# First weights converted through PSUM, gated inputs and squared keys on ScalarE and GpSimd alone, attention output evicted by VectorE

## The chip, the cores and the metric

The kernel runs on one core of a Trainium2 chip. Its engines are TensorE (PE in the profile; PEld is its weight load), VectorE (DVE), ScalarE (ACT), GpSimd (POOL) and SyncE (SP), whose queue issues the DMAs. The metric is the device time of one execution in microseconds (us).

## The reference: what is computed

Three blocks follow each other, for batch 4, sequence 576 and model width 512.

- Attention with 8 heads of 64: rotary embedding of q and k, scores `q k^T / 8`, softmax, product with v.
- A gated feed-forward: with `x_prev` the input shifted by one position, `xk = mu_k*x + (1-mu_k)*x_prev` and `xr` alike with `mu_r`; `k = relu(xk @ w_k)`; `out = sigmoid(xr @ w_r) * ((k*k) @ w_v)`, with d_ff = 1024.
- A mixer: `u = x + (relu(x^T @ w_tok1) @ w_tok2)^T`, then `u + relu(u @ w_ch1) @ w_ch2`, with 256 token and 1536 channel features.

The weights w_k, w_v, w_r, w_tok and w_ch arrive as 64-bit floats; q, k, v and mu as 32-bit floats.

## The kernel before, in words

Every matrix product of 32-bit values is made of three matmuls: each operand is split into a high part in the matmul's own format and a low part, the rest, and high*high, high*low and low*high are summed (`mm3`, L527 to L532). So every operand needs one rounding copy and one subtraction. A 288-column half of the 576 positions is the moving operand in most products.

**Conversion of weights (`Conv`).** A weight is taken in chunks of 128 x 512 values, each two 32-bit words. Stage 0 loads the chunk by a DMA. Stage 1 has ScalarE write the absolute value of the high word into a work tile `cv` (L191). Stage 2 is four VectorE operations on it: clamp (L196), mask and shift (L198), sign and exponent bits out of the high word (L200), low bits out of the low word (L202). Stage 3 rounds on ScalarE (`parts`, L73) and subtracts (`parts`, L104) on the engine that `low` names. `conv0` does the 16 chunks of w_k and w_v beside the attention, `conv1` the 11 chunks of w_r and the token weights near the end of the attention, `conv2` the 24 chunks of the channel weights after it. One `step` issues stages for two chunks.

**Attention.** There are 16 groups (batch x pair of heads), each with 9 softmax tiles of 128 rows; tile j has the scores `S` (L362), the negated maximum `nm` (L368, DVE), the exp in place in PSUM (L375, ACT), the reciprocal of the sum (L382, L383, DVE), the probabilities as two 16-bit halves `p` (high on ACT, L75, low on DVE, L394), a DMA transpose (L411) and, for each of two units per group, the product with v (`pv`, L424). `out` (L433) evicts that product, scaled, from PSUM into `xT`. The rotary embedding of the next group's k (`rk`) and q (`rq`) is three elementwise steps each (`rope`), on DVE or POOL. `prep` issues it.

**Feed-forward (`kvr_gen`).** It starts once the first batch of attention is done and runs as a stream between the tiles of the later groups. A unit `K` is one batch and one half: `lerp_slice` makes the gated input in four slices (`a`, `f`, then `xs` high and low; the pools of `a` and `f` have one buffer each), eight products `kp` follow, each evicted with relu (`t`, L599), squared (`q`, L603), rounded (`k`, L80) and subtracted (`k`, L104), and then four products `vp` over all eight squared keys. A unit `R` does the gate for batch 0. `tok_gen` is the token mixing, `ch_gen` the channel mixing (`c1p`, `co`), `gate_gen` the gate of the later batches.

**Order.** The program is written as one stream; a scheduler with a timeline of its own and the priorities in `PRI` sets the order in which each engine's instructions stand. Each engine then runs its list strictly in that order. In POOL's list the 16 `words` memsets of `conv0` stand behind a rotary step and hold back the weight loads. The helper `copy` (L73 to L82) and `tt` (L104) record most elementwise work, so the profile tells such work apart by the names of the tiles and not by the line.

At two places the order of the change speaks for itself.

The first is VectorE's list in the second attention group, where `conv0` runs. `cv` and `cvp` are the work tiles of the conversion, `parts` the low half of a weight, `p16` the low half of the probabilities, `nm` the maximum. Before:

```order
L196 TENSOR_SCALAR cv_775<-cv_775 128x512
L202 SCALAR_TENSOR_TENSOR cv_683<-words_565,cv_683 128x512
L368 TENSOR_REDUCE nm_491<-S_478 128x1
L196 TENSOR_SCALAR cv_777<-cv_777 128x512
L308 TENSOR_REDUCE va_537<-vps_511 1x1
L104 TENSOR_TENSOR parts_889<-cv_681,parts_889 128x512
L198 TENSOR_SCALAR cv_775<-cv_775 128x512
L368 TENSOR_REDUCE nm_514<-S_501 128x1
L104 TENSOR_TENSOR parts_892<-cv_683,parts_892 128x512
```

With the change:

```order
L200 SCALAR_TENSOR_TENSOR cvp_578<-words_453,cvp_578 128x512
L402 SCALAR_TENSOR_TENSOR p16_622<-S_543,rc_618,p16_622 128x576
L376 TENSOR_REDUCE nm_616<-S_600 128x1
L335 COPY sc_609<-vps2_607 128x2
L203 SCALAR_TENSOR_TENSOR cv_583<-words_453,cvp_578 128x512
L376 TENSOR_REDUCE nm_637<-S_627 128x1
L390 TENSOR_SCALAR den_640<-S_600 128x1
L376 TENSOR_REDUCE nm_714<-S_676 128x1
L196 TENSOR_SCALAR cvp_690<-cvp_690 128x512
```

Before, several chunks are in work at once; now a chunk runs from its clamp to its last operation before the next begins, with more attention rows between, and no `parts` stands on this engine. The sixteenth chunk's last VectorE operation stood behind 15 tiles' `p16` rows and stands behind 31 now.

The second is POOL's list in the first `K` unit, where `k2` is a rounded or subtracted squared key. Before:

```order
L104 TENSOR_TENSOR k2_1743<-q_1725,k2_1743 128x288
L104 TENSOR_TENSOR kq_1957<-rk_1565,kq_1956 128x576
L104 TENSOR_TENSOR rq_3053<-rq_3053,tab_151 128x640
L104 TENSOR_TENSOR rk_2981<-rk_2981,tab_151 128x576
L104 TENSOR_TENSOR k2_1775<-q_1761,k2_1775 128x288
```

With the change:

```order
L104 TENSOR_TENSOR q_1738<-t_1731 128x288
L104 TENSOR_TENSOR k2_1736<-q_1738,k2_1736 128x288
L104 TENSOR_TENSOR kq_1982<-rk_1584,kq_1981 128x576
L104 TENSOR_TENSOR q_1773<-t_1766 128x288
L104 TENSOR_TENSOR k2_1771<-q_1773,k2_1771 128x288
```

Each key now takes two rows of this engine, the square and the subtraction, with the rotary rows of later groups between them as before.

## Time and profile before

| what | us |
|---|---|
| median of 3 runs | 1050.69 (1049.54 to 1056.28) |
| the profiled execution | 1050.36 |
| its span | 1048.6 |
| busy in the span: PE, PEld | 908.0, 831.5 |
| busy in the span: DVE, ACT, POOL | 628.7, 485.5, 391.6 |

The span is what the trace covers; 1.8 us of the profiled execution lie around it. Busy time is a sum over stages that differ, so the rows below are cut by stage. Groups 0, 2, 4 and 5 of the attention begin with an exp near 21, 122, 176 and 204 us, and the last exp begins at 512.6 us. A duration in the trace includes some 0.07 us in which the next instruction of the engine already runs: a row that starts at 48.62 us and takes 0.41 us is followed by one that starts at 48.96 us.

### The profile page before, as it was taken

The numbers are of one execution on the slowest core, as the hardware profiler recorded it, in microseconds if no ns is written. First come the engines' busy times: TensorE is split into PE (matmuls) and PEld (weight loads), VectorE is DVE, ScalarE is ACT, GpSimd is POOL, SyncE is SP. The second block draws the span as 40 slices with busy tenths as digits, with TensorE's granted clock in tenths as the row PEclk, the third lists the DMA queues.
The fourth block names the chain that finished last, engine by engine and source line by source line (L and its number), as shares of the span: only waits on it lengthen the run. The fifth ranks groups of instructions, "written<-read, shape, count | busy, mean of one in ns | idle before, by whom it ended". The sixth has DMA issues, their size and how long they took to land.

```text
span 1048.6 us, 17649 instructions
## 1 busy us (share of the span) xinstructions
PE 908.0 (87%) x6544; PEld 831.5 (79%) x6544; DVE 628.7 (60%) x1306; ACT 485.5 (46%) x1080; POOL 391.6 (37%) x383
## 2 busy tenths in 40 slices
PE   2433676899999999998888988899999999999998
PEld 1322555678887788887688887899999999999997
DVE  7999777777867878787784379933313312231111
ACT  3535556676766767785653455433233112211110
POOL 6275344465655644133263555441132012201010
PEclk9999556799998999998999997999999999999999
DMA  8974578878888887887840156010020002000000
GB/s 271 315 185 111 117 148 183 173 161 190 169 189 169 163 168 136 152 186 153 188 158 29 58 193 259 1 47 24 1 91 24 24 1 75 1 24 1 24 23 24
DMA packets 212054, 120.80 MB, mean 115 GB/s; under 512 B 175232, under 2 KB 192768, under 8 KB 211840
## 3 DMA queue, kind: packets, MB, share of 16 engines
q1 hardware_dynamic: 211968, 119.67, 48.0%
q8 instruction: 52, 0.85, 0.3%
q14 instruction: 34, 0.28, 0.1%
HBM read 60.90 MB, written 14.16 MB: 72 GB/s over the span
## 4 chain that ended last, share of the span: by engine, by line
PE 48%; DVE 10%; issue 2%; DMA 2%; POOL 2%; ACT 1%; SPq 0%; DVEq 0%; POOLq 0%; ACTq 0%
PE c1p L530 5%; PE c1p L531 5%; PE c1p L532 5%; PE co L531 5%; PE co L530 4%; PE co L532 4%; PE S L362 3%; DVE cv L196 2%; DVE cv L200 2%; DVE cv L202 2%; PE vp L530 2%; PE vp L531 1%; PE vp L532 1%; PE pv L424 1%; PE rp L530 1%
## 5 line engine op out<-in xcount | busy, mean ns | idle before, releaser
L362 PE MATMUL S<-kq 64*128 64x288 f32 (+1 forms) x864 | 153.0, 346 | 49.7 <-DVE p L394 39.0
L362 PEld LDWEIGHTS S<-kq 64*128 64x128 f32 (+1 forms) x864 | 125.1, 219 | 73.6 <-issue 39.5
L375 ACT ACTIVATE S<-S,nm 128x576 f32<-128x576 f32 x144 | 102.3, 715 | 73.6 <-DVE nm L368 72.3
L869 DVE SCALAR_TENSOR_TENSOR hs<-c1p,hs 128x288 fp32r<-128x288 f32 x96 | 43.5, 455 | 152.7 <-ACT hs L868 152.7
L368 DVE TENSOR_REDUCE nm<-S 128x1 f32<-128x576 f32 x144 | 106.4, 749 | 32.7 <-PE S L362 32.3
L394 DVE SCALAR_TENSOR_TENSOR p<-S,rc,p 128x576 f16<-128x576 f32 x144 | 113.7, 809 | 15.0 <-ACT p L75 13.9
L530 PE MATMUL c1p<-uhl,parts 128*128 128x288 f32 x384 | 115.0, 301 | 6.5 <-DVE hs L869 3.3
L868 ACT ACTIVATE hs<-c1p 128x288 fp32r<-128x288 f32 x96 | 38.8, 409 | 173.3 <-PE c1p L532 169.9
L531 PE MATMUL c1p<-uhl,parts 128*128 128x288 f32 x384 | 114.5, 299 | 0.0
L532 PE MATMUL c1p<-uhl,parts 128*128 128x288 f32 x384 | 114.5, 299 | 0.0
L532 PE MATMUL co<-hs,parts 128*128 128x288 f32 x384 | 113.8, 298 | 0.0
L531 PE MATMUL co<-hs,parts 128*128 128x288 f32 x384 | 113.3, 297 | 0.0
L75 ACT ACTIVATE p<-S,rc 128x576 f16<-128x576 f32 x144 | 104.2, 751 | 18.0 <-ACT S L375 5.8
L530 PE MATMUL co<-hs,parts 128*128 128x288 f32 x384 | 110.2, 299 | 0.3 <-DVE y L104 0.3
L104 POOL TENSOR_TENSOR uhl<-y,uhl 128x288 fp32r<-128x288 f32 x32 | 26.1, 840 | 200.5 <-ACT uhl L73 200.3
L104 POOL TENSOR_TENSOR k<-q,k 128x288 fp32r<-128x288 f32 x64 | 54.4, 852 | 123.2 <-DVE k L80 85.0
L530 PE MATMUL kp<-xs,parts 128*128 128x288 f32 x256 | 82.9, 331 | 12.2 <-ACT t L599 6.6
L530 PE MATMUL vp<-k,parts 128*128 128x288 f32 x256 | 79.6, 313 | 3.8 <-ACT vt L73 3.0
L424 PE MATMUL pv<-pt,vh 128*64 128x256 f16 (+1 forms) x576 | 59.4, 334 | 26.1 <-DMA pt<-p 24.5
L530 PEld LDWEIGHTS c1p<-uhl,parts 128*128 128x128 f32 x384 | 73.4, 192 | 7.7 <-DVE hs L869 4.3
L531 PE MATMUL kp<-xs,parts 128*128 128x288 f32 x256 | 78.6, 309 | 0.7 <-POOL xs L104 0.6
L531 PE MATMUL vp<-k,parts 128*128 128x288 f32 x256 | 78.2, 307 | 0.5 <-POOL k L104 0.5
(112 smaller groups left out, 2384.2 us busy)
## 6 DMA issues: line engine op xcount, KB each, us to landing
words<-in_w_c_dram SPq DMA_DIRECT2D x24, 512.0 KB, 7.2
rq<-in_qin_dram SPq DMA_DIRECT2D x32, 320.0 KB, 3.5
rk<-in_kin_dram SPq DMA_DIRECT2D x32, 288.0 KB, 3.5
vr<-in_vw_dram SPq DMA_DIRECT2D x16, 320.0 KB, 3.3
xd<-xT SPq DMA_DIRECT2D x16, 288.5 KB, 2.9
vd<-vt SPq DMA_DIRECT2D x32, 144.0 KB, 2.3
y<-vd SPq DMA_DIRECT2D x8, 576.0 KB, 4.8
out_dram<-y SPq DMA_DIRECT2D x8, 576.0 KB, 3.5
```

The costliest lines, as they stand in the source:

```text
L75: act.activation(out=o, in_=i, func=AF.Copy, scale=scale)
L104: return (pool if e == "P" else dve).tensor_tensor(o, a, b, op=op)
L362: pe.matmul(p[:, h, 0:HS], lhsT=a[l, 128 * m:128 * m + 128], rhs=b[l, h * HS:(h + 1) * HS], start=(n == 0), stop=(n == 2))
L368: dve.tensor_reduce(out=nm, in_=S_t[j][:, :, 0:HS], op=ALU.max, axis=AX.XY, negate=True)
L375: act.activation(out=e, in_=e, func=AF.Exp, bias=sum_t[j], accum_out=s)
L394: dve.scalar_tensor_tensor(out=t[:, 1], in0=S_t.pop(j)[:, :, 0:HS], scalar=sum_t[j], in1=t[:, 0], op0=ALU.mult, op1=ALU.subtract)
L424: pe.matmul(p[l, 0:n], lhsT=v[:, a, l], rhs=ts[x][:, c, :], start=(i == 0), stop=(i == len(prods) - 1))
L530: pe.matmul(p, lhsT=wh, rhs=t[:, 0], start=first, stop=False)
L531: pe.matmul(p, lhsT=wh, rhs=t[:, 1], start=False, stop=False)
L532: pe.matmul(p, lhsT=wl, rhs=t[:, 0], start=False, stop=last)
L868: act.activation(out=h[:, 0], in_=p[:, 0:HS], func=AF.Relu)
L869: dve.scalar_tensor_tensor(out=h[:, 1], in0=p[:, 0:HS], scalar=0.0, in1=h[:, 0].bitcast(F32), op0=ALU.max, op1=ALU.subtract)
```

## The change

- `conv0` gets a `room`: its work tile is a PSUM tile `cvp` in the pool of the accumulators (one buffer, idle while `conv0` runs). Only the fourth VectorE operation writes back to an SBUF tile `cv`. Its stages follow each other chunk by chunk, loads two steps ahead. Its subtraction moves from DVE to POOL; that of `conv1` and `conv2` moves from POOL to DVE.
- `lerp_slice`: POOL scales the shifted input, ACT the input, POOL adds; ACT rounds, POOL subtracts. No step is left on DVE.
- The squared key: ACT squares straight into the rounded half; POOL squares once more and subtracts. No step is left on DVE.
- The attention output is evicted by DVE in place of ACT.
- The rotary embedding of k for groups 1 to 4 is on POOL wholly; two of three steps were on DVE.

```diff
-            def __init__(self, cv, weights, name, load=None, low="P"):
-                self.cv, self.name, self.load, self.low = cv, name, load, low
+            def __init__(self, cv, weights, name, load=None, low="P", room=None):
+                self.cv, self.name, self.load, self.low, self.room = cv, name, load, low, room
...
                 if j == 1:
-                    v = self.t[i] = self.cv()[:, :w]
+                    v = self.t[i] = (self.room or self.cv)()[:, :w]
...
-                    yield lambda: dve.scalar_tensor_tensor(out=v, in0=lw, scalar=29, in1=v,
+                    o = self.t[i] = self.cv()[:, :w] if self.room else v
+                    yield lambda: dve.scalar_tensor_tensor(out=o, in0=lw, scalar=29, in1=v,
                                                            op0=ALU.logical_shift_right, op1=ALU.bitwise_or)
...
                 with ahead(PRI.get(self.name, 0)):
+                    if self.room:
+                        for d in range(2):
+                            for j in (3, 1, 2, 0):
+                                for f in self.stage(j, n + d - (0, 2, 2, 4)[j]):
+                                    if f is not None:
+                                        f()
+                        return
...
-                act.activation(out=xT[b][:, pr, 1 + t0:1 + t0 + n], in_=p[:, 0:n], func=AF.Copy,
-                               scale=sc_t[g][:, 1:2])
+                copy("D", xT[b][:, pr, 1 + t0:1 + t0 + n], p[:, 0:n], sc_t[g][:, 1:2])
...
-                    rope(g, 0, n, "DDP"[n] if g <= NP else "P")
+                    rope(g, 0, n, "P")
...
-            copy("PA"[w], a, x[:, kk, o:o + HS], om_s[:, w, kk:kk + 1])
+            copy("P", a, x[:, kk, o:o + HS], om_s[:, w, kk:kk + 1])
             f = P["f"].tile([128, HS], F32, tag="f", name="f")
-            dve.scalar_tensor_tensor(out=f, in0=x[:, kk, o + 1:o + HS + 1], scalar=mu_s[:, w, kk:kk + 1], in1=a,
-                                     op0=ALU.mult, op1=ALU.add)
+            copy("A", f, x[:, kk, o + 1:o + HS + 1], mu_s[:, w, kk:kk + 1])
+            tt("P", f, f, a, ALU.add)
             t = P["xs"].tile([128, 2, HS], F32R, tag="xs", name="xs")
-            copy("AP"[w], t[:, 0], f)
-            tt("PD"[w], t[:, 1], f, t[:, 0].bitcast(F32), ALU.subtract)
+            copy("A", t[:, 0], f)
+            tt("P", t[:, 1], f, t[:, 0].bitcast(F32), ALU.subtract)
...
-                            t, k2[m] = k2[m], P["q"].tile([128, HS], F32, tag="q", name="q")
-                            act.activation(out=k2[m], in_=t, func=AF.Square)
-
-                        def ev3(m=m):
-                            q, k2[m] = k2[m], P["k2"].tile([128, 2, HS], F32R, tag="k2", name="k2")
-                            copy("D", k2[m][:, 0], q)
+                            t, k2[m] = k2[m], P["k2"].tile([128, 2, HS], F32R, tag="k2", name="k2")
+                            act.activation(out=k2[m][:, 0], in_=t, func=AF.Square)
+                            q = P["q"].tile([128, HS], F32, tag="q", name="q")
+                            tt("P", q, t, t, ALU.mult)
                             tt("P", k2[m][:, 1], q, k2[m][:, 0].bitcast(F32), ALU.subtract)
-                        later((1, ev1), (3, ev2), (5, ev3))
+                        later((1, ev1), (2, ev2))
...
         cv = Conv(lambda: P["xs"].tile([128, 2 * HS], I32, tag="xs", name="cv"),
-                  wk + wv, "conv0", "rope", "D")
+                  wk + wv, "conv0", "rope", "P", lambda: acc_p.tile([128, 512], I32, tag="acc", name="cvp"))
...
-        cv = Conv(cv_t, [wr, t1, t2], "conv1")
+        cv = Conv(cv_t, [wr, t1, t2], "conv1", low="D")
...
-        cv = Conv(cv_t, [w for ws in zip(c1_w, c2_w) for w in ws], "conv2")
+        cv = Conv(cv_t, [w for ws in zip(c1_w, c2_w) for w in ws], "conv2", low="D")
```

## Rows read from the trace of the kernel before

**Rows 1.** Windows, core 0: stretch, us, busy (count) per engine, PEclk, DMA share, GB/s.

```profile
21.00:122.00 101.00, 41.71 (x199) 31.95 (x200) 98.84 (x186) 52.55 (x99) 51.68 (x40) 0.91 0.68 189
122.00:176.00 54.00, 39.46 (x230) 30.65 (x228) 36.73 (x85) 30.04 (x63) 23.72 (x18) 0.61 0.85 171
...
204.00:505.00 301.00, 286.98 (x2158) 246.29 (x2159) 234.99 (x541) 210.43 (x464) 141.47 (x135) 0.95 0.83 167
505.00:612.00 107.00, 95.21 (x688) 88.08 (x687) 62.51 (x114) 50.85 (x125) 53.41 (x64) 0.98 0.36 102
612.00:687.00 75.00, 63.51 (x422) 61.12 (x421) 72.13 (x110) 36.80 (x75) 39.08 (x31) 0.89 0.40 153
```

**Rows 2.** Lines by form, VectorE, 21 to 122 us: busy, mean ns, idle before.

```profile
L104 DVE TENSOR_TENSOR parts<-cv,parts 128x512 fp32r<-128x512 f32 x16 | 14.5, 908 | 0.0
L394 DVE SCALAR_TENSOR_TENSOR p<-S,rc,p 128x576 f16<-128x576 f32 x18 | 14.3, 801 | 0.6 <-ACT p L75 0.6
L200 DVE SCALAR_TENSOR_TENSOR cv<-words,cv 128x512 int32<-128x512 int32 x16 | 14.2, 885 | 0.0
L368 DVE TENSOR_REDUCE nm<-S 128x1 f32<-128x576 f32 x19 | 14.0, 744 | 1.5 <-PE S L362 1.4
L196 DVE TENSOR_SCALAR cv<-cv 128x512 f32<-128x512 f32 x16 | 12.3, 770 | 0.0
L202 DVE SCALAR_TENSOR_TENSOR cv<-words,cv 128x512 int32<-128x512 int32 x16 | 12.1, 757 | 0.0
L198 DVE TENSOR_SCALAR cv<-cv 128x512 int32<-128x512 int32 x16 | 9.5, 600 | 0.0
L104 DVE TENSOR_TENSOR rk<-rk,tab 128x576 f32<-128x576 f32 x4 | 4.4, 1110 | 0.0
```

**Rows 3.** Timeline of VectorE, 48 to 61 us: start, duration, instruction.

```profile
48.62 0.41 DVE L196 TENSOR_SCALAR cv<-cv 128x512 f32<-128x512 f32 x1
...
52.94 2.02 DVE L104 TENSOR_TENSOR parts<-cv,parts 128x512 fp32r<-128x512 f32 x1
54.88 0.74 DVE L368 TENSOR_REDUCE nm<-S 128x1 f32<-128x576 f32 x1
...
58.98 1.75 DVE L196 TENSOR_SCALAR cv<-cv 128x512 f32<-128x512 f32 x1
60.65 0.67 DVE L200 SCALAR_TENSOR_TENSOR cv<-words,cv 128x512 int32<-128x512 int32 x1
```

**Rows 4.** Timeline of GpSimd, the same stretch.

```profile
52.70 3.66 POOL L104 TENSOR_TENSOR rq<-rq,tab 128x640 f32<-128x640 f32 x2
...
58.40 1.98 POOL L104 TENSOR_TENSOR rq<-rq 128x640 f32<-128x640 f32 x1
```

**Rows 5.** Lines by form, GpSimd, 204 to 505 us.

```profile
L104 POOL TENSOR_TENSOR k<-q,k 128x288 fp32r<-128x288 f32 x40 | 33.7, 843 | 101.3 <-DVE k L80 69.0 <-DVE den L382 19.9 <-PE S L362 5.5
...
L104 POOL TENSOR_TENSOR rk<-rk,tab 128x576 f32<-128x576 f32 x13 | 18.6, 1428 | 5.9 <-DMA rk<-in_kin_dram 5.9
```

**Rows 6.** Lines by form, VectorE, 612 to 687 us.

```profile
L196 DVE TENSOR_SCALAR cv<-cv 128x512 f32<-128x512 f32 x20 | 18.1, 907 | 0.3 <-ACT cv L191 0.3
L202 DVE SCALAR_TENSOR_TENSOR cv<-words,cv 128x512 int32<-128x512 int32 x20 | 17.4, 872 | 0.0
L200 DVE SCALAR_TENSOR_TENSOR cv<-words,cv 128x512 int32<-128x512 int32 x20 | 16.8, 839 | 0.2
L198 DVE TENSOR_SCALAR cv<-cv 128x512 int32<-128x512 int32 x20 | 12.5, 626 | 0.0
...
L104 DVE TENSOR_TENSOR y<-t2p,y 128x288 f32<-128x288 f32 x7 | 3.1, 448 | 0.4 <-PE t2p L759 0.3
```

**Rows 7.** Lines by form, GpSimd, 612 to 687 us.

```profile
L104 POOL TENSOR_TENSOR parts<-cv,parts 128x512 fp32r<-128x512 f32 x20 | 28.8, 1442 | 32.6 <-ACT parts L73 32.4
```

**Rows 8.** Lines by form of the whole run.

```profile
L520 DVE SCALAR_TENSOR_TENSOR f<-xT,mu_s,a 128x288 f32<-128x288 f32 x40 | 30.8, 770 | 17.2 <-POOL xs L104 9.8 <-POOL a L77 6.8
...
L75 ACT ACTIVATE a<-x,om_s 128x288 f32<-128x288 f32 x24 | 12.7, 527 | 2.9 <-DMA x<-xd 2.1 <-DVE f L829 0.7
```

## The prediction

> **What bounds the kernel now.** I read the busy time by stretch first, since one limit does not hold for the whole span. From 21 to 122 us VectorE is busy 98.84 of 101 us, while TensorE works 41.71 [rows 1]: two attention groups and the 16 chunks of the first conversion run here, and VectorE sets the end. From 122 to 176 us two further groups run without a conversion. Nothing is full there (VectorE 36.73 of 54, the DMA engines 0.85), and the loop from scores to transposed probabilities and back keeps a pace of 54 / 18 = 3.0 us per softmax tile. From 204 to 505 us the feed-forward fills TensorE: 286.98 of 301 us [rows 1], so at most 14 us are to be had. From 505 to 612 us TensorE is busy 95.21 of 107. From 612 to 687 us the last conversion holds VectorE again, 72.13 of 75 [rows 1]. The rest is TensorE alone.
>
> Next I looked inside the first stretch. The clamp of a chunk takes 0.41 us at 48.62 and 1.75 us at 58.98; a subtraction takes 2.02 us at 52.94 [rows 3]. The long ones lie beside GpSimd's work at 52.70 and 58.40 [rows 4], the short one beside none. The maximum over a PSUM tile keeps its 0.74 us at 54.88 in the middle of GpSimd's pair [rows 3, 4], and the two forms that read PSUM average 0.801 and 0.744 over the stretch [rows 2]. So operations between SBUF tiles wait for GpSimd, those with a PSUM input don't.
>
> **The change, part by part.** Successive rows overlap by some 0.07 us (48.62 plus 0.41 against a next start at 48.96), which I take off each.
>
> *First conversion.* Removed: five operations per chunk of 0.770 + 0.600 + 0.885 + 0.757 + 0.908 = 3.92 us [rows 2], 16 times 62.7 us, less 80 overlaps 57.1 us. Added: four operations that have one operand in PSUM. No row shows VectorE writing PSUM. The nearest that read it are 0.448 us for 288 columns [rows 6] and 0.801 for 576 [rows 2]; 512 columns between them give 0.71. Lower end 0.41 (the free clamp, rows 3), upper end 0.80. I take 0.70, nearest to the PSUM rows: 64 times 0.63 is 40.3 us. Saved: 16.8 us, with the ends 10 and 35.
>
> The Trainium skill speaks against this step: "VectorE: DVE Perf Modes", section "Why PSUM operands drop a tier", says that a 32-bit operand in PSUM costs the doubled rate that SBUF to SBUF has. By it the free clamp and mask become 0.29 us longer, 32 times 9 us of VectorE, and only the end of the waiting pays for it; without the rule the stretch would give some 10 us more than below. The PSUM rows above agree with it as far as reads go.
>
> *Also on VectorE from 21 to 176 us:* four rotary products go, 4 times 1.04 us = 4.2 [rows 2]; three `f` of 0.770 go, 2.1 [rows 8]; seven evictions come, 0.45 each by the 288-column row, 2.7 [rows 6]. Busy time goes from 98.84 + 36.73 = 135.6 to 135.6 - 16.8 - 4.2 - 2.1 + 2.7 = 115.2 us.
>
> *What that does to the end.* In the order, the conversion now lasts through 31 tiles, not 15. Attention costs VectorE 36.73 / 18 = 2.04 us per tile, so 31 tiles and the conversion make 31 x 2.04 + 40.3 = 103.5 us, against the loop's own 31 x 3.0 = 93. VectorE stays the bound, but barely, and its idle time in the loop (a third) can't all be filled in a fixed order. I assume 90% busy, between 68% (122 to 176) and 98% (21 to 122): 115 us, and 5 tiles at 3.0 behind them, 130 us in place of 155. **-25 us.** The DMA engines allow it: they are busy 0.68 x 101 + 0.85 x 54 = 114.6 us of these 155 [rows 1], 88% of 130; that is also why I go no further than -31. Lower end, at 0.80 per operation and 85% density: -13.
>
> *What GpSimd gets there.* 16 subtractions of 1.442 us [rows 7], 23 us, and eight rotary products of 1.428 [rows 5], 11 us, on top of 51.68 + 23.72 us of 155 [rows 1]: 110 of 130 us. It is not the bound, since its own long rows were waits for VectorE too (1.98 us for a rotary row at 58.40, rows 4), but a key's low half for the next group now stands behind subtractions. Cost 0, inside the 90%.
>
> *Gated inputs and keys, 204 to 505 us.* VectorE loses 40 roundings and 20 `f`, and GpSimd gains 40 squares of 0.843 [rows 5] and 20 sums of the same size, 51 us: 141.47 + 51 = 192 of 301 us, 64%. TensorE hides both. **0**, between -8 and +10. ScalarE trades the evictions for scaled copies of 0.527 [rows 8]; at 210.43 of 301 us it covers them.
>
> *505 to 612 us.* A slice's chain replaces a 0.770 us operation with 0.527 on ScalarE and 0.843 on GpSimd [rows 5, 8], 0.6 us longer, and single buffers make slices queue. A gate unit is 48 matmuls of 286.98 / 2158 = 0.133 us [rows 1], 6.4 us, shorter than its four slices; twelve slices (two gate units and the unit behind them) are late by 7 us, of which I let token matmuls hide half. A key takes GpSimd 1.69 us and TensorE 12 x 0.133 = 1.60, so two units outside the attention lose another 1. **+5**, between 0 and +12.
>
> *612 to 687 us.* The four operations average 0.907 + 0.626 + 0.839 + 0.872 = 3.24 us [rows 6]; free they take 0.41, 0.41, 0.67 and 0.67 [rows 3], so 20 chunks carry 21.6 us of waiting. GpSimd loses 28.8 of its 39.08 us here [rows 1, 7]; a quarter of the waiting stays, -16. The subtraction joins VectorE, 20 times 0.60 = +12. **-4**, between -7 and +2 (subtractions as long as 0.908, rows 2).
>
> *Sum:* -25 + 0 + 5 - 4 = -24 on the profiled 1050.4, so 1026 us. The median is 0.3 us above that execution, which changes nothing. The ends, taken as independent of each other (root of the squares: 12, 10, 7 and 6 upward, 6, 8, 5 and 3 downward), make the likeliest case 1014 to 1044.
>
> **The rivals.**
>
> *GpSimd becomes the bound (slower).* Eight keys per unit, each with one more product of 0.843 [rows 5], are 6.7 us; eight units that hold the second product's matmuls back for all of it cost 54 us: 1080. For it: in the group in which a unit's keys are made, 16 rows of 0.843 and seven rows of the attention of at least 1.4 us stand in one list, some 24 of 27 us. Against it: 64% over the stretch, and a unit needs its keys only as the second product reaches them. It decides, above 1061, once more than two thirds of these 54 us are exposed. The Trainium skill sides with this rival: "GPSIMD Engine Reference", section "Engine selection", keeps elementwise work of two inputs on VectorE since GpSimd needs about twice as long; 0.843 against 0.448 for 288 columns [rows 5, 6] agrees.
>
> *PSUM in place costs double.* If reading and writing one PSUM bank halves the pace, 48 operations gain some 0.6 us each, 29 us of VectorE, and at 90% the first stretch is 32 us longer: 1058. Nothing in the trace speaks for it or against it: no row has VectorE write PSUM.
>
> *One bank stalls ScalarE.* The next chunk's first step must wait until the last chunk has left the bank, and exps stand behind it: at 1 us a chunk 16 us, 1042.
>
> *More than forecast.* With VectorE free of gating, the loop itself gets faster than 3.0 us per tile, and 204 to 505 us gains its 14: 1008.
>
> **How the numbers follow.** Forecast 0.67; GpSimd 0.09, of which some only reaches 1050; double PSUM 0.07; one bank 0.09; more 0.08. The time is the forecast's, 1026. The range, 1010 to 1047, leaves out the double price, the worse part of GpSimd and half of the best case. One per cent, 10.5 us, is what a measurement of this kernel can tell from no change. Faster by more, below 1040: the best case and the forecast without its slow edge of 0.06, 0.69, and 0.01 of the others, 0.70; slower by more, above 1061: most of GpSimd and the bad end of the double price, 0.08; within: 0.22.
>
> **What would show it.** Right: the four conversion rows near 0.7 us with or without GpSimd beside them; the 37th exp near 150 us in place of 176; VectorE about 90% busy until the conversion ends; 204 to 505 us of the old trace moved but as long; the last conversion at some 3.0 us of VectorE per chunk and GpSimd half idle there. Wrong: conversion rows above 1 us (double price); TensorE waiting for `k` from GpSimd in the feed-forward, and its count per us below 7 there (GpSimd bound); ScalarE idle before the first conversion step (one bank). If the 37th exp moves but the end doesn't, the gain was lost between 204 and 612 us.

## The result, and the profile after

| | before | after |
|---|---|---|
| median, us | 1051.28 (4 runs, 1049.54 to 1056.28) | **1012.02** (1011.16 to 1013.54) |
| ratio | 1 | 0.9621 [0.9585, 0.9656] |
| profiled execution, its span | 1050.36, 1048.6 | 1011.27, 1009.5 |

The change gains 39 us. The forecast was 24; the time lies inside the range, near its fast end, and 2 us below the likeliest case's own range. It is nearer to the 1008 us of the rival "more than forecast" than to the forecast's 1026, but what that rival names, a gain in the feed-forward, did not come.

I cut both traces at the same five events: the 37th exp (first of group 4), the last exp, the first clamp of the last conversion, the first channel product `c1p`, the end. The forecast's last two terms meet at 612 us, where the last conversion begins; its first clamp is therefore the mark for them, and `c1p` lies 28 to 30 us behind it. The events of the kernel after, from the timelines of ScalarE, VectorE and TensorE (columns: start us, us, engine, line, operation, out<-in, count, idle time before it and its releaser):

```profile
144.14 0.71 ACT L383 ACTIVATE S<-S,nm 128x576 f32<-128x576 f32 x1
...
481.07 0.71 ACT L383 ACTIVATE S<-S,nm 128x576 f32<-128x576 f32 x1
...
583.44 0.43 DVE L196 TENSOR_SCALAR cv<-cv 128x512 f32<-128x512 f32 x1 [0.69 <-ACT cv L191]
...
611.79 0.41 PE L537 MATMUL c1p<-uhl,parts 128*128 128x288 f32 x1 [3.71 <-DVE y L104]
```

Before, the exps were at 176.1 and 512.6 us, and the clamp and `c1p` here by the timelines of VectorE and TensorE:

```profile
614.05 0.64 DVE L196 TENSOR_SCALAR cv<-cv 128x512 f32<-128x512 f32 x1 [0.27 <-ACT cv L191]
...
644.26 0.61 PE L530 MATMUL c1p<-uhl,parts 128*128 128x288 f32 x1 [3.12 <-DVE y L104]
```

| stretch | before | after | measured | forecast |
|---|---|---|---|---|
| start to 37th exp | 176.1 | 144.1 | -32.0 | -25 |
| to the last exp | 336.5 | 336.9 | +0.4 | 0 |
| to the first clamp of the last conversion | 101.5 | 102.4 | +0.9 | +5 |
| to the end of the span | 434.5 | 426.0 | -8.5 | -4 |

Cut at `c1p` instead, the last two are 131.7 and 130.7 us (-1.0), and 404.3 and 397.7 us (-6.6). Of the first stretch's 32 us, 1.3 fell before the first exp (21.4 and 20.1 us).

Busy time of the kernel after by stretch (from:to, length, then busy us and count of PE, PEld, DVE, ACT, POOL, the granted clock, the mean share of the 16 DMA engines, which reaches 1.13 in e9 below, and GB/s), which answers to [rows 1]:

```profile
20.00:54.00 34.00, 17.91 (x89) 14.51 (x88) 31.06 (x68) 20.89 (x42) 21.70 (x28) 1.00 1.02 266
54.00:87.00 33.00, 20.77 (x116) 17.14 (x116) 30.13 (x73) 19.95 (x41) 28.93 (x26) 0.59 1.02 299
...
20.00:144.00 124.00, 76.10 (x428) 59.94 (x427) 113.97 (x249) 78.02 (x158) 94.51 (x87) 0.74 0.93 229
...
172.00:473.00 301.00, 287.54 (x2175) 244.37 (x2174) 218.50 (x513) 211.20 (x467) 182.40 (x195) 0.98 0.83 167
...
580.00:655.00 75.00, 67.43 (x487) 66.50 (x486) 69.76 (x132) 41.17 (x86) 17.09 (x19) 0.95 0.43 159
...
481.00:612.00 131.00, 108.95 (x760) 101.00 (x759) 68.89 (x128) 68.86 (x159) 77.80 (x99) 0.97 0.48 156
```

VectorE is busy 113.97 of 124 us (92%) up to the 37th exp, where 115.2 of 130 was forecast. TensorE is as full in the feed-forward as before, 287.54 of 301. GpSimd has 182.40 us there in place of 141.47, and 17.09 in place of 39.08 in the last conversion.

The first conversion, by line on VectorE from 20 to 144 us (busy us, mean ns, idle before), in place of [rows 2]:

```profile
L198 DVE TENSOR_SCALAR cvp<-cvp 128x512 int32<-128x512 int32 x16 | 11.1, 692 | 0.2
L196 DVE TENSOR_SCALAR cvp<-cvp 128x512 f32<-128x512 f32 x16 | 11.0, 688 | 0.6 <-ACT cvp L191 0.6
L200 DVE SCALAR_TENSOR_TENSOR cvp<-words,cvp 128x512 int32<-128x512 int32 x16 | 11.0, 685 | 0.0
L203 DVE SCALAR_TENSOR_TENSOR cv<-words,cvp 128x512 int32<-128x512 int32 x16 | 10.8, 676 | 0.0
```

Two of them in the timeline of VectorE of the kernel after, as in [rows 3]:

```profile
54.54 0.69 DVE L198 TENSOR_SCALAR cvp<-cvp 128x512 int32<-128x512 int32 x1
...
55.87 0.69 DVE L200 SCALAR_TENSOR_TENSOR cvp<-words,cvp 128x512 int32<-128x512 int32 x1
```

GpSimd's timeline beside them, as in [rows 4]:

```profile
53.87 1.26 POOL L104 TENSOR_TENSOR parts<-cv,parts 128x512 fp32r<-128x512 f32 x1 [3.43 <-ACT parts L73]
...
56.87 1.41 POOL L104 TENSOR_TENSOR rk<-rk,tab 128x576 f32<-128x576 f32 x1 [1.74 <-DMA rk<-in_kin_dram]
```

The mask at 54.54 lies beside GpSimd's subtraction (53.87 to 55.13) but for its last 0.1 us, the next operation at 55.87 beside none, and both take 0.69 us. Before, the clamp took 0.41 us alone and 1.75 us beside GpSimd [rows 3, 4]. The free operation got dearer, the contended one much cheaper.

Squared keys on GpSimd from 172 to 473 us, by line, as in [rows 5]:

```profile
L104 POOL TENSOR_TENSOR k<-q,k 128x288 fp32r<-128x288 f32 x42 | 35.0, 835 | 6.9 <-ACT k L610 3.4 <-issue 1.1 <-POOL q L104 1.0
L104 POOL TENSOR_TENSOR q<-t 128x288 f32<-128x288 f32 x42 | 30.8, 734 | 46.0 <-ACT t L606 43.2 <-PE pv L432 2.6
```

What TensorE waited for in the same 301 us (us in total, times, longest):

```profile
PE pv L432 <- DMA pt<-p: 5.7, 4, 3.2
...
PE vp L538 <- POOL k L104: 0.7, 1, 0.7
```

TensorE waits 0.7 us for a key of GpSimd. The last conversion on VectorE from 580 to 655 us, in place of [rows 6]:

```profile
L203 DVE SCALAR_TENSOR_TENSOR cv<-words,cv 128x512 int32<-128x512 int32 x20 | 14.5, 741 | 0.0
L200 DVE SCALAR_TENSOR_TENSOR cv<-words,cv 128x512 int32<-128x512 int32 x20 | 14.2, 712 | 0.0
L104 DVE TENSOR_TENSOR parts<-cv,parts 128x512 fp32r<-128x512 f32 x20 | 13.7, 684 | 0.1
L198 DVE TENSOR_SCALAR cv<-cv 128x512 int32<-128x512 int32 x20 | 10.8, 546 | 0.0
L196 DVE TENSOR_SCALAR cv<-cv 128x512 f32<-128x512 f32 x20 | 9.9, 499 | 0.8 <-ACT cv L191 0.7
```

Five operations now take 3.18 us per chunk; the four took 3.24 [rows 6]. From its first clamp to the end of its last subtraction the conversion lasts 71.2 us, and lasted 72.4. What changed beside it is TensorE, in the first of these windows before and in the second after:

```profile
614.00:687.00 73.00, 61.51 (x407) 59.12 (x406) 70.70 (x107) 35.81 (x74) 37.33 (x29) 0.88 0.39 146
...
583.50:655.00 71.50, 63.93 (x460) 63.00 (x459) 68.20 (x130) 39.65 (x82) 13.68 (x14) 0.95 0.40 151
```

TensorE does 460 matmuls beside the conversion in place of 407, is idle for 7.6 us in place of 11.5, and its mean granted clock is 0.95 in place of 0.88. At 0.133 us each, 53 matmuls are by estimate 7.0 us that no longer stand behind the conversion. Of the 3.9 us of idle time that went, 3.3 were waits for the eviction `hs` of a channel product on VectorE, here in the list of TensorE's waits from 614 to 687 us before, which has no such row from 583.5 to 655 us after:

```profile
PE c1p L530 <- DVE hs L869: 3.3, 2, 2.1
```

### The profile page after: what moved, and what is told of

It reads as the page before. It is cut to its first block, busy times and chain, and to the rows that moved or that the text cites. A ratio compares the mean times of both kernels' runs of the same rounds, so it can differ in the third digit from the quotient of the medians.

```text
span 1009.5 us, 17679 instructions
## 1 busy us (share of the span) xinstructions
PE 897.5 (89%) x6544; PEld 822.2 (81%) x6544; DVE 566.3 (56%) x1237; ACT 487.9 (48%) x1088; POOL 445.5 (44%) x484
## 4 chain that ended last, share of the span: by engine, by line
PE 55%; DVE 5%; DMA 3%; POOL 2%; ACT 2%; issue 1%; SPq 0%; DVEq 0%; POOLq 0%; ACTq 0%
PE c1p L537 5%; PE co L537 5%; PE c1p L538 5%; PE c1p L539 5%; PE co L538 5%; PE co L539 5%; PE S L370 4%; PE pv L432 2%; PE vp L537 2%; PE kp L537 2%; PE vp L538 2%; PE vp L539 2%; PE rp L537 1%; PE rp L538 1%; PE rp L539 1%; PE kp L539 1%
## 5 line engine op out<-in xcount | busy, mean ns | idle before, releaser
L383 ACT ACTIVATE S<-S,nm 128x576 f32<-128x576 f32 x144 | 102.2, 713 | 66.9 <-DVE nm L376 66.1
L537 PE MATMUL c1p<-uhl,parts 128*128 128x288 f32 x384 | 114.6, 299 | 3.7 <-DVE y L104 3.7
L539 PE MATMUL co<-hs,parts 128*128 128x288 f32 x384 | 112.6, 296 | 0.0
L538 PE MATMUL co<-hs,parts 128*128 128x288 f32 x384 | 112.5, 296 | 0.0
L537 PE MATMUL co<-hs,parts 128*128 128x288 f32 x384 | 107.7, 296 | 0.0
L537 PE MATMUL kp<-xs,parts 128*128 128x288 f32 x256 | 79.8, 322 | 14.6 <-ACT xs L73 7.3
L537 PE MATMUL vp<-k,parts 128*128 128x288 f32 x256 | 79.1, 313 | 2.1 <-ACT vt L73 1.1
L538 PE MATMUL vp<-k,parts 128*128 128x288 f32 x256 | 78.0, 306 | 0.7 <-POOL k L104 0.7
L538 PE MATMUL kp<-xs,parts 128*128 128x288 f32 x256 | 76.5, 301 | 1.7 <-POOL xs L104 1.4
L539 PE MATMUL vp<-k,parts 128*128 128x288 f32 x256 | 77.8, 305 | 0.0
L104 POOL TENSOR_TENSOR q<-t 128x288 f32<-128x288 f32 x64 | 46.4, 729 | 68.9 <-ACT t L606 66.1
```

The lines of the kernel that those rows point to most:

```text
L104: return (pool if e == "P" else dve).tensor_tensor(o, a, b, op=op)
L383: act.activation(out=e, in_=e, func=AF.Exp, bias=sum_t[j], accum_out=s)
L537: pe.matmul(p, lhsT=wh, rhs=t[:, 0], start=first, stop=False)
L538: pe.matmul(p, lhsT=wh, rhs=t[:, 1], start=False, stop=False)
L539: pe.matmul(p, lhsT=wl, rhs=t[:, 0], start=False, stop=last)
```

## The experiments

Each expectation states the theory it tests and the rival it sets against it. The experiments stand on three chips, on which the kernel before took 1043.8, 1047.6 and 1053.8 us, so totals are compared as ratios to before; stretches are from one profiled execution each. Every edit also gives the scheduler another timeline, so the lists of a variant differ from the change's in more places than the edit. Two executions of the change have the 37th exp at 144.1 and 146.2 us, and e8 and e11 (below), with as much work on VectorE up to there, have it at 149.6 and 148.0; so a difference below some 5 us there says little.

### Where the first stretch's 32 us come from

**e1, the same work tile in SBUF.** The order of a chunk's stages and the engines are the change's; the scheduler's lists differ (25 tiles' `p16` rows stand ahead of the conversion's last row, not 31).

```diff
+        cvp_p = right("cvp", 1)
...
-                  wk + wv, "conv0", "rope", "P", lambda: acc_p.tile([128, 512], I32, tag="acc", name="cvp"))
+                  wk + wv, "conv0", "rope", "P", lambda: cvp_p.tile([128, 512], I32, tag="cvp", name="cvp"))
```

> The changed kernel with one thing altered: the work tile of the first conversion lies in SBUF again (one buffer of its own), in the same order of stages and with the same engines. Theory A (PSUM pays because VectorE no longer waits for GpSimd): the first two rows of a chunk fall to 0.41 us where GpSimd is idle, but all four wait where it is busy, which is three quarters of 20 to 144 us; their mean goes from 0.685 to 0.85 to 1.0 us, 64 rows lose 11 to 20 us, the 37th exp moves from 144 to 153 to 162 us and the time to 1022 to 1032 us. Theory B (what pays is that work left VectorE and that chunks follow each other): the mean falls below 0.685 and the time is 1012 or a few us less.

Measured: 1033.53, ratio 0.987 [0.9836, 0.9904]; 37th exp at 171.8. VectorE by line, 21 to 172 us:

```profile
L200 DVE SCALAR_TENSOR_TENSOR cvp<-words,cvp 128x512 int32<-128x512 int32 x16 | 19.7, 1231 | 0.2
L203 DVE SCALAR_TENSOR_TENSOR cv<-words,cvp 128x512 int32<-128x512 int32 x16 | 17.6, 1100 | 0.1
L198 DVE TENSOR_SCALAR cvp<-cvp 128x512 int32<-128x512 int32 x16 | 17.2, 1076 | 0.3
L196 DVE TENSOR_SCALAR cvp<-cvp 128x512 f32<-128x512 f32 x16 | 15.1, 946 | 0.5 <-ACT cvp L191 0.4
```

Four operations of 4.35 us in place of 2.74, 16 times 1.61 = 26 us more of VectorE, and the 37th exp is 27.7 us later, more than theory A's range (mean 1.09 us, 0.85 to 1.0 expected). So the new order of the stages without PSUM does not bring the gain. How much of the 27.7 us is the scheduler's other list is not shown; the longer rows account for 26. The Trainium skill, "SBUF — State Buffer", section "SBUF: two separate sides", describes a port pair that VectorE and GpSimd share as an exclusive lock, held for a whole instruction; these rows agree (1.231 us with two SBUF inputs, 0.685 with one of them in PSUM).

**e2, the first conversion as before, the rest of the change kept**, and **e3, the kernel before with the conversion edit alone** (the diff of `Conv` and of its `conv0` call).

```diff
-                  wk + wv, "conv0", "rope", "P", lambda: acc_p.tile([128, 512], I32, tag="acc", name="cvp"))
+                  wk + wv, "conv0", "rope", "D")
```

> The changed kernel with the first conversion as before the change (SBUF tile, two chunks side by side, subtraction on VectorE). Theory A: it is worth nearly all of the first stretch, so 25 us of its 32 come back, the 37th exp is near 169 us and the time 1035 to 1042 us. Theory B (rotary steps, gated inputs and evictions carry as much): less than half comes back, 1020 to 1027 us.

> The kernel before with the change of the first conversion alone. Theory A: the 37th exp falls from 176 to about 150 us and the time to 1022 to 1030 us. Theory B: the rotary steps of groups 1 to 4 still stand on VectorE and GpSimd is not the only cause, so less than half is gained, 1035 to 1045 us.

Measured: e2 1033.53, 0.9882 [0.9841, 0.9922], 37th exp at 177.3. e3 1027.88, 0.9825 [0.9782, 0.9867], 37th exp at 153.7. The first window of e2, to be read beside the first of [rows 1]:

```profile
21.00:122.00 101.00, 38.57 (x193) 30.77 (x194) 99.48 (x170) 50.44 (x93) 56.26 (x48) 0.93 0.69 186
```

The conversion alone gives 22.4 us of the stretch; everything else alone gives nothing there (177.3 against 176.1), and 9.6 us on top of the conversion. With the old conversion VectorE stays 98% busy in e2, though the rotary steps and gated inputs have left it. By its ratio e2's total is 0.9882 of the result's 1051.28 us, 1039 us, inside theory A's range, but not as theory A has it: the first stretch loses 33 us and not 25, and from the 37th to the last exp the profiled execution took 322.1 us where before and after take 336.5 and 336.9 and the other runs with the change's feed-forward 331 to 339, though no instruction of that stretch is on another engine than in the change. An order of the lists that is worth some 10 us there may exist; I did not isolate it.

**e5, two of three rotary steps of k back on VectorE for groups 1 to 4**, and **e6, the eviction back on ScalarE.**

```diff
-                    rope(g, 0, n, "P")
+                    rope(g, 0, n, "DDP"[n] if g <= NP else "P")
```

```diff
-                copy("D", xT[b][:, pr, 1 + t0:1 + t0 + n], p[:, 0:n], sc_t[g][:, 1:2])
+                act.activation(out=xT[b][:, pr, 1 + t0:1 + t0 + n], in_=p[:, 0:n], func=AF.Copy,
+                               scale=sc_t[g][:, 1:2])
```

> The changed kernel with two of the three rotary steps of k for groups 1 to 4 on VectorE again. The first conversion alone left the 37th exp at 153.7 us, the whole change has it at 144.1. Theory A (VectorE, 92% busy, is still the bound of the first stretch, and these eight products of 1.0 to 1.3 us are most of the 10 us between): 37th exp at 149 to 154 us, time 1016 to 1022 us. Theory B (the DMA engines, full from 20 to 87 us, are the bound now): 37th exp at 143 to 146 us, time 1010 to 1014 us.

> The changed kernel with the attention output evicted by ScalarE again. Theory A (VectorE is the bound up to the 37th exp): seven rows of 0.5 us leave it there, 37th exp 2 to 4 us earlier, time 1008 to 1011 us. Theory B (ScalarE's list is the tighter one, since the eviction waits for the product and exps stand behind it): 37th exp 2 us later or more and the feed-forward stretch longer, 1015 to 1022 us.

Measured: e5 1016.21, 0.9717 [0.9666, 0.9768], 37th exp at 150.6, some 5 us after that of e6 and e7 on the same chip (145.4, 145.8), but 1 us after that of e8 (149.6). Up to there VectorE has 121.43 us of work, in e7 116.22:

```profile
20.00:150.00 130.00, 83.12 (x432) 64.45 (x431) 121.43 (x261) 79.38 (x159) 85.64 (x77) 0.72 0.92 222
```

And the window of e7:

```profile
20.00:146.00 126.00, 76.71 (x427) 60.38 (x425) 116.22 (x251) 77.80 (x159) 94.31 (x84) 0.73 0.94 226
```

The 5.2 us put back on VectorE agree with theory A in size. They don't show it, since e8 is as late with 115.37 us of work in its first 130:

```profile
20.00:150.00 130.00, 76.74 (x425) 60.30 (x425) 115.37 (x259) 75.94 (x155) 93.44 (x81) 0.72 0.92 219
```

e6 1015.69, 0.9746 [0.9664, 0.9827]: VectorE has 112.69 us of work up to 146 us, 3.5 less than in e7, and the 37th exp is no earlier, against theory A. The interval lies above the change's 0.9621 and overlaps that of e12, the change on another chip (0.9652); the eviction's place is not settled.

**e9, every chunk of the first conversion loaded twice**, **e10, the first conversion's clamp left out** (the output lacks the clamp of those weights), and **e12, the change itself on the same chip.**

```diff
-                    sp.dma_start(raw if wide else raw[:, :w], src.bitcast(I32))
+                    for _ in range(2 if self.room else 1):
+                        sp.dma_start(raw if wide else raw[:, :w], src.bitcast(I32))
```

```diff
-                    yield lambda: dve.tensor_scalar(out=v.bitcast(F32), in0=v.bitcast(F32), scalar1=F64_LEAST,
-                                                    scalar2=F64_MOST, op0=ALU.max, op1=ALU.min)
+                    if not self.room:
+                        yield lambda: dve.tensor_scalar(out=v.bitcast(F32), in0=v.bitcast(F32), scalar1=F64_LEAST,
+                                                        scalar2=F64_MOST, op0=ALU.max, op1=ALU.min)
```

> The changed kernel, each of the 16 chunks of the first conversion loaded twice into the same tile: 8.4 MB more for the DMA engines, which are full from 20 to 87 us (share 1.02, 282 GB/s), so some 28 us of their time. Theory A (the DMA engines are the bound of that stretch now): 37th exp 15 to 28 us later, time 1025 to 1040 us. Theory B (VectorE, 92% busy, is): 37th exp at most 6 us later, time up to 1018 us.

> The changed kernel without the clamp of the first conversion, 16 rows of 0.69 us or 10 us of VectorE less (it leaves out the guard for values beyond the 32-bit range). Theory B (VectorE is the bound from 20 to 144 us): 37th exp at 134 to 138 us, time 1000 to 1005 us. Theory A (the DMA engines are): 37th exp at 141 to 145 us, time 1008 to 1013 us.

> The changed kernel itself on the chip of the three others, to compare with: 0.958 to 0.966 of the kernel before, 37th exp within 2 us of 144, stretches as in its first trace within 3 us.

Measured: e12 1015.16, 0.9652 [0.9614, 0.969], 37th exp at 146.2; e9 1025.13, 0.9753 [0.9697, 0.9808], 149.9; e10 1013.39, 0.9625 [0.9587, 0.9664], 148.3. Windows of e12, and their sum from 20 to 150 us:

```profile
87.00:116.00 29.00, 16.21 (x103) 12.08 (x101) 26.12 (x51) 18.05 (x37) 26.19 (x20) 0.68 0.87 178
116.00:150.00 34.00, 24.32 (x133) 18.98 (x134) 30.59 (x75) 22.05 (x45) 20.99 (x18) 0.65 0.79 157
sum 130.00, PE 78.51 PEld 62.19 DVE 117.21 ACT 80.42 POOL 96.63; mean PE 19.63 PEld 15.55 DVE 29.30 ACT 20.10 POOL 24.16
```

Windows of e9:

```profile
20.00:54.00 34.00, 16.34 (x88) 13.80 (x88) 31.61 (x78) 22.35 (x46) 20.78 (x24) 0.95 1.07 279
...
87.00:116.00 29.00, 19.02 (x112) 15.27 (x111) 28.11 (x60) 18.65 (x37) 13.11 (x15) 0.57 1.13 305
116.00:150.00 34.00, 22.78 (x122) 16.61 (x120) 29.23 (x63) 20.66 (x43) 30.95 (x23) 0.70 1.08 240
```

The sum of e10 over the same stretch:

```profile
sum 130.00, PE 79.21 PEld 59.86 DVE 108.83 ACT 80.70 POOL 95.02; mean PE 19.80 PEld 14.96 DVE 27.21 ACT 20.18 POOL 23.76
```

In e9 the DMA share is 1.06 to 1.13 for all 130 us, and the 37th exp is 3.7 us later: the doubled bytes go into the room after 87 us. That is theory B's reading, though the total, 1% above e12, is not in its range. In e10 VectorE has 8.4 us less to do (108.83 against 117.21 in e12) and the 37th exp does not come earlier; both theories missed. But e10 is not e12 less the clamp. Its lists end the conversion 23 us sooner, with fewer tiles beside it; the last operation of the sixteenth chunk in e10 and in e12:

```profile
109.02 0.68 DVE L204 SCALAR_TENSOR_TENSOR cv<-words,cvp 128x512 int32<-128x512 int32 x1
...
131.67 0.68 DVE L203 SCALAR_TENSOR_TENSOR cv<-words,cvp 128x512 int32<-128x512 int32 x1
```

Ahead of it stand the `p16` rows of 22 tiles in e10 and of 31 in e12, and the tiles that are left of the 36 go at the loop's own pace. The prediction's sum, end of the conversion plus 3.0 us for each tile left, gives 109.0 + 14 x 3.0 = 151.0 us for e10 (148.3 measured), 131.7 + 5 x 3.0 = 146.7 for e12 (146.2), and for the kernel before, with 15 tiles ahead of 112.2 us, 175.2 (176.1). Over all runs it is at most 1.3 us too low (e11) and 6.4 too high (e1). So, as far as this sum goes, two things set the 37th exp: when VectorE is through with the conversion, and how many tiles the lists put beside it. e1 shows the first. e10 doesn't show that less work on VectorE is worth nothing, since the second changed with it; and whether the DMA engines, at a share of 1.02 up to 87 us, hold the conversion back in the change itself stays open.

### Where the rest comes from

**e4, the subtraction of the two later conversions back on GpSimd.**

```diff
-        cv = Conv(cv_t, [wr, t1, t2], "conv1", low="D")
+        cv = Conv(cv_t, [wr, t1, t2], "conv1")
...
-        cv = Conv(cv_t, [w for ws in zip(c1_w, c2_w) for w in ws], "conv2", low="D")
+        cv = Conv(cv_t, [w for ws in zip(c1_w, c2_w) for w in ws], "conv2")
```

> The changed kernel with the subtraction of the second and third conversion on GpSimd again. Theory A (in the last conversion VectorE waits for GpSimd's subtractions): the stretch from the first channel product to the end grows back by 4 to 7 us, time 1016 to 1019 us. Rival: the stretch is bound by the weight loads or by the chain of a chunk, and shortens if VectorE has one operation fewer: 1005 to 1012 us.

Measured: 1026.54, 0.9805 [0.977, 0.984]. From the last exp to `c1p` 136.8 us (+6.1), from there to the end 403.8 (+6.1), as theory A has it. Cut at the first clamp of the last conversion it is 105.2 (+2.8) and 435.4 (+9.4). Seven other runs that have the change's arrangement there (e1, e2, e5, e6, e9, e10, e12) take 426.4 to 428.4 us for the second part, and the kernel before and e3 434.5 and 436.7. For the first part six of the seven take 102.2 to 104.0, and e6 106.4, so +2.8 isn't clear. VectorE by line, 580 to 660 us:

```profile
L200 DVE SCALAR_TENSOR_TENSOR cv<-words,cv 128x512 int32<-128x512 int32 x20 | 19.9, 1000 | 0.2
L203 DVE SCALAR_TENSOR_TENSOR cv<-words,cv 128x512 int32<-128x512 int32 x20 | 18.6, 936 | 0.1
```

The two operations with two SBUF inputs are 0.2 to 0.3 us longer than after. Beside the last conversion TensorE falls back to 399 matmuls, and its waits for `hs` are there again:

```profile
585.70:659.00 73.30, 58.84 (x399) 55.38 (x398) 71.63 (x107) 35.95 (x74) 38.91 (x30) 0.93 0.38 145
...
PE c1p L537 <- DVE hs L874: 4.5, 5, 1.3
```

So the place of the subtraction, which e4 moves in the conversion before (`conv1`) as well, brings all of that stretch's gain. In total it is worth 12 us by the profiled executions, of which e4's is the fastest of its four, and 16 to 19 by the ratios (0.9805 against 0.9652 and 0.9621), above the 1016 to 1019 us of theory A.

**e7, squared keys as before, e8, gated inputs as before, e11, both mixed:** keys as before, gated inputs of the `R` units as before, those of the `K` units as in the change. The first diff is the keys' of e7 and e11, the second the gated inputs' of e11; e8 has the branch `if w` for every unit.

```diff
-                            t, k2[m] = k2[m], P["k2"].tile([128, 2, HS], F32R, tag="k2", name="k2")
-                            act.activation(out=k2[m][:, 0], in_=t, func=AF.Square)
-                            q = P["q"].tile([128, HS], F32, tag="q", name="q")
-                            tt("P", q, t, t, ALU.mult)
+                            t, k2[m] = k2[m], P["q"].tile([128, HS], F32, tag="q", name="q")
+                            act.activation(out=k2[m], in_=t, func=AF.Square)
+
+                        def ev3(m=m):
+                            q, k2[m] = k2[m], P["k2"].tile([128, 2, HS], F32R, tag="k2", name="k2")
+                            copy("D", k2[m][:, 0], q)
...
-                        later((1, ev1), (2, ev2))
+                        later((1, ev1), (3, ev2), (5, ev3))
```

```diff
-            copy("P", a, x[:, kk, o:o + HS], om_s[:, w, kk:kk + 1])
+            copy("PA"[w], a, x[:, kk, o:o + HS], om_s[:, w, kk:kk + 1])
...
-            copy("A", f, x[:, kk, o + 1:o + HS + 1], mu_s[:, w, kk:kk + 1])
-            tt("P", f, f, a, ALU.add)
+            if w:
+                dve.scalar_tensor_tensor(out=f, in0=x[:, kk, o + 1:o + HS + 1], scalar=mu_s[:, w, kk:kk + 1],
+                                         in1=a, op0=ALU.mult, op1=ALU.add)
+            else:
+                copy("A", f, x[:, kk, o + 1:o + HS + 1], mu_s[:, w, kk:kk + 1])
+                tt("P", f, f, a, ALU.add)
...
-            copy("A", t[:, 0], f)
-            tt("P", t[:, 1], f, t[:, 0].bitcast(F32), ALU.subtract)
+            copy("AP"[w], t[:, 0], f)
+            tt("PD"[w], t[:, 1], f, t[:, 0].bitcast(F32), ALU.subtract)
```

> The changed kernel with the squared keys as before (square on ScalarE, rounding on VectorE, one subtraction on GpSimd). Theory A (TensorE bounds the feed-forward stretch, both ways are hidden): 37th exp unchanged, that stretch 330 to 338 us, time 1009 to 1015 us. Rival (the rounding copy waits for GpSimd and delays the attention's own VectorE rows): stretch above 340 us, time above 1018 us.

> The changed kernel with the gated inputs as before (sum on VectorE). Theory A (a slice's chain is 0.6 us longer with the change, and single buffers queue it): the stretch from the last exp to the first channel product shrinks by 3 to 6 us from 131, the rest is unchanged, time 1006 to 1011 us. Rival (freeing VectorE of these operations, which wait for GpSimd, is worth more than the chain): time 1014 to 1020 us.

> The changed kernel with the squared keys as before, and the gated inputs of the R units alone (batch 0's gate) as before; the K units' gated inputs stay on ScalarE and GpSimd. Theory A (from 540 to 560 us GpSimd, 17 of 20 us busy, sets the pace of the gate units, and the keys' second product costs 8 us after the attention): the stretch from the last exp to the first channel product falls from 131 to 112 to 118 us, the feed-forward stretch stays at 333 to 340, time 12 to 18 us below the changed kernel's. Rival (what was gained there is lost by VectorE's waits, as with the gated inputs undone altogether, or by the order the scheduler finds): within 5 us of the changed kernel.

Measured:

| | time, ratio | 37th to last exp | last exp to `c1p` |
|---|---|---|---|
| change | 1012.02, 0.9621 [0.9585, 0.9656] | 336.9 | 130.7 |
| e7 | 1007.42, 0.9638 [0.959, 0.9685] | 338.2 | 122.4 |
| e8 | 1013.18, 0.9678 [0.9604, 0.9753] | 350.6 | 116.7 |
| e12 (change again) | 1015.16, 0.9652 [0.9614, 0.969] | 335.9 | 131.9 |
| e11 | **1005.00**, 0.955 [0.9517, 0.9582] | 337.1 | 120.4 |

The stretch from the last exp to `c1p` in windows (that of the change is above, 481 to 612 us). In e4:

```profile
480.00:617.00 137.00, 111.24 (x762) 101.61 (x760) 71.91 (x111) 69.36 (x160) 99.99 (x117) 0.96 0.43 146
```

In e7:

```profile
484.00:606.00 122.00, 105.68 (x746) 97.98 (x745) 67.30 (x141) 67.38 (x156) 66.23 (x80) 0.99 0.46 151
```

In e8:

```profile
500.00:617.00 117.00, 104.98 (x748) 98.89 (x747) 80.07 (x148) 60.73 (x141) 59.81 (x75) 0.97 0.50 170
```

In e11:

```profile
485.00:606.00 121.00, 105.72 (x751) 98.46 (x750) 78.69 (x161) 64.59 (x148) 52.97 (x64) 0.99 0.47 157
```

TensorE has much the same work in all, 105 to 111 us. With 99.99 us on GpSimd the stretch takes 137 us, with 77.80 it takes 131, with 53 to 66 us 117 to 122. The kernel before doesn't fit this row: there GpSimd has 69.97 us, VectorE 89.37, and the stretch takes 131.7. In this stretch the change's keys and gates cost 8 and 14 us against the change's profile, 130.7; the seven other runs that leave keys and gates as in the change, e4 aside, take 130.7 to 134.9 there. In the totals neither shows by itself: the ratios of e7 and e8 have the change's within their intervals. Inside the attention the keys cost nothing (e7). e8's old gates make that stretch 13.7 us longer in its profile, which is the slowest of four executions (1002.86 to 1017.49 us); e11's old gates, of the `R` units alone, don't. That fits the `K` units' gates gaining there by being off VectorE, but e2 shows as much from an order alone, so it isn't shown. e11 takes each edit where it helped and is 10 us faster than the change on the same chip, with intervals that don't meet, less than the 12 to 18 us expected. It is the fastest version, faster than both kernels.

## Why the prediction was right, and where its sizes were off

- **First stretch, -25, measured -32.** The mechanism was right. The rows came at 0.685 us (0.70 taken), the same with or without GpSimd, and e1 shows that the place of the tile brings this. VectorE's work was forecast at 115.2 us and is 113.97. What was mis-sized is the density: 92% in place of 89. The lower end of -13 should have been -11 ((31 x 2.04 + 64 x 0.73) / 0.85 + 15 = 144 us in place of 155), which moves the slow end of the likeliest case from 1044 to 1046 us. The Trainium skill's tier rule ("VectorE: DVE Perf Modes", "Why PSUM operands drop a tier") holds for PSUM writes too by these rows, 0.688 us against 0.41 for the free clamp in SBUF, and the end of the waiting paid for it as worked out.
- **"No further than -31."** The DMA engines' work was sized right, 114.6 us forecast and 0.93 x 124 = 115.3 measured; I held that 88% was as full as they would be, and they ran at 1.02 for 67 us.
- **"VectorE stays the bound."** Not settled. e1's 26 us on it come with an end 27.7 us later, and the sum of conversion and remaining tiles fits before, e10 and e12 within 3 us. e10 took 8.4 us away and gained nothing, but in another order.
- **204 to 505 us, 0.** Right, +0.4: TensorE 287.54 of 301 us and 0.7 us of waiting for GpSimd's keys. The rival in which GpSimd becomes the bound fell. e8 and e2 hint that the 0 may hide a gain of the gates; the sum of it is right, its parts aren't shown.
- **505 to 612 us, +5, measured +0.9.** Inside its range of 0 to +12. From the last exp to the first clamp of the last conversion the old arrangement took 101.5 us (before) and 99.0 (e3), the new one 102.4, and 102.2 to 104.0 in six other runs. The parts were sized too small: with the old keys it takes 97.8 us (e7), with the old gates 87.7 (e8), with e11's mixture 95.8, so 4.6, 14.7 and 6.6 us less than the change in place of the 1 and 4 forecast. Something gives most of that back. The forecast left out that the subtraction of `conv1` leaves GpSimd here, but the 2.8 us that e4 puts on it are hardly clear of the spread, so what it is stays open.
- **612 to 687 us, -4, measured -8.5.** This step failed, outside its range of -7 to +2. It took VectorE's time for the conversion to be the time of the stretch. That time hardly moved: 3.18 us a chunk (3.0 expected), and 71.2 us from first clamp to last subtraction in place of 72.4. What the step left out is TensorE beside it, which gets 53 more matmuls done, by estimate 7.0 us of the 8.5. e4 ties this to the subtraction on GpSimd: with it back, 399 matmuls and the old 435 us. TensorE waited for `hs` on VectorE, 3.3 us before, none after, 4.5 in e4, and the granted clock was 0.88 before and 0.95 after; how the two share the 7.0 us isn't shown.
- **The total.** Three terms missed on the same side, by 7, 4 and 4.5 us, and with them the time came within 2 us of the range's fast end. That it is still inside is in part luck.
- **The other rivals.** Double price fell (0.69 in place). One bank stalling ScalarE is there in the list of ScalarE's waits from 20 to 144 us, 12.9 us of the 16 that the rival priced:

```profile
ACT cvp L191 <- DVE cv L203: 12.9, 5, 3.8
```

It cost little, since ScalarE is busy 78.02 of these 124 us and VectorE, whose clamps come next, waited 0.6 us for it (`ACT cvp L191` in the first conversion's rows).

## What to carry to other kernels

Where VectorE works beside a busy GpSimd, look at the same operation's duration with and without a GpSimd row beside it; if they differ, try an idle PSUM bank as work tile. Here each operation then cost its PSUM price, 0.68 to 0.69 us, beside GpSimd or not, and the 26 us of shorter rows showed in the end of the stretch. Look also at how many rows of the following work stand beside the bound engine's: what is left behind it goes at its own pace. Price a move between engines for each stretch apart: the keys on GpSimd were free while TensorE was full and cost some 8 us in the stretch after the attention. And don't size a stretch by its fullest engine alone: the last conversion took as long as before, and the gain was the work that TensorE got done beside it.

## What the runs showed of the hardware

VectorE worked in place in one PSUM tile without a penalty: 0.685 us for 512 columns with one input in SBUF, read and written in PSUM, against 0.676 where the same kind of operation wrote to SBUF. On GpSimd a product of a 128x288 tile with itself took 0.734 us, a subtraction of two tiles of that size 0.835. GpSimd's own rows became shorter too when the first conversion's tile left SBUF: its subtraction takes 1.387 us in e1 and 1.286 after, and the rotary product took the first of these times before (21 to 122 us) and the second after (20 to 144 us), where its whole mix of neighbours had changed:

```profile
L104 POOL TENSOR_TENSOR rq<-rq,tab 128x640 f32<-128x640 f32 x9 | 19.9, 2223 | 11.9 <-DMA rq<-in_qin_dram 11.9
...
L104 POOL TENSOR_TENSOR rq<-rq,tab 128x640 f32<-128x640 f32 x14 | 22.1, 1585 | 3.1 <-DMA rq<-in_qin_dram 3.1
```
